# Moving the skip term into the lag-0 tap, generating masters in blocks of 3 and 5 chunks, and splitting the table sums: a kernel of gated attention and state-space convolution

## The chip, the cores and the metric

The kernel runs on one core of one Trainium2 chip. The metric is the device time of one execution in microseconds (us). A kernel was run several times in each round, and the medians below are over its runs, all of one state (no run stood out as slow). A profile was taken of one execution of each kernel. In it PE is TensorE (PEld its weight loads), DVE is VectorE, ACT is ScalarE, POOL is GpSimd, SP is SyncE, whose instruction stream issues most DMAs here. L977 is line 977 of that kernel's file, and so the same statement has other line numbers in another kernel.

## The reference, cut to what matters

```python
x = A_x                                        # 2048 tokens x 448
g = sigmoid((x * gate_w).sum(-1, keepdims=True))
# branch a: 16 query heads of 28, one key and one value head for all
q, k, v = x @ wq, x @ wk, x @ wv
a = softmax(q k^T / sqrt(28)) v @ wo
# branch b: a convolution along the tokens, one kernel K of length 2048 for each channel
dt = exp(log_dt); logdA = dt * (A_re + i A_im)             # 448 channels x 256 states
K[d, l] = Re( sum_n C[d,n] * exp(logdA[d,n] * l) * dt*B[d,n] )
y = causal_convolution(x, K)
b = y + x * Dskip                                          # the skip term
return g * a + (1 - g) * b
```

The skip term `x * Dskip` is a convolution with a kernel that is `Dskip` at lag 0 and zero elsewhere. So it may as well be added to `K[:, 0]`.

## The kernel before

Attention and convolution run side by side. The attention makes 410 batches of scores (two or three tiles of 128 keys x 512 queries). TensorE writes the scores to PSUM (the memory for its results), ScalarE takes the exponential, and TensorE multiplies with the values. The convolution works on 28 chunks of 16 channels. For each one, VectorE builds tables of powers, TensorE multiplies them to the kernel K ("kernel generation"), K goes to DRAM and comes back as a Toeplitz matrix `T`, and TensorE convolves. VectorE then multiplies by 1-g into `cst` (this I call the eviction). TensorE transposes that, and VectorE adds it to `O`, the output of all tokens in SBUF (the core's working memory).

**A list scheduler makes the order.** The program declares operations with an assumed duration and a priority. At build time a simulation picks, again and again, the operation that can start first, and in case of a tie the one of lower priority number. This fixes each engine's instruction order before the program runs; where an operation isn't ready in time, its engine waits:

```python
def el(n, rate=0.96, fix=69):          # assumed ns of a VectorE operation on n elements
    return fix + n / rate
class Prog:
    SEM_NS = 60                        # assumed ns for a semaphore to reach another engine
    SLACK = {"pe": 500.0, "dve": 300.0}
    SWITCH = 107.0                     # assumed ns when TensorE changes its tiling
    def schedule(self):
        ...
        while done < n:
            for e in ENG:
                for i in ready[e]:
                    r = max(rt[i], free[e])
                    ...
                    key = (r, o.pr, i)
                    if best is None or key < best[0]:
                        best = (key, e, i)
```

The code below is shortened: access patterns and bookkeeping are cut.

**Masters** are the powers exp(dt·A·2^k), k = 0 to 10, by repeated squaring in float32, for a block of four chunks at once. Each power is cast to bf16, and a negated copy of its imaginary part is written beside it:

```python
def masters(self, b):                       # sizes = [4] * 7
    for k in range(11):
        if k:
            tensor_tensor(msq, src_both(k-1), src_both(k-1), mult)          # 2*BW elements, BW = 128
            tensor_tensor(mst re, msq re, msq im, subtract)                 # BW
            scalar_tensor_tensor(mst im, src re, 2.0, src im, mult, mult)   # BW
        tensor_copy(mbf ..., src_both(k))                                   # 2*BW, float32 to bf16
        tensor_scalar(mbf ..., src im, -1.0, mult)                          # BW, the negated copy
```

**Tables** double five times for each chunk: two multiplies and one sum over n = 128, 256, 512, 1024 and 2048 elements.

```python
        tensor_tensor(d, a, mbf re, mult)        # n
        tensor_tensor(tmp, a, mbf im/-im, mult)  # n
        tensor_tensor(d, d, tmp, add)            # n: the negated copy makes one addition of both halves
```

**The skip term and the end of the program:**

```python
def skip(self):
    pg.dma(x and B_Dskip -> SBUF)                                      # 1.8 MB
    for i in range(16):                                                # 128 tokens each
        scalar_tensor_tensor(tv, tv, (1 - g), Dskip, mult, mult)       # 448 elements
        tensor_tensor(ov, ov, tv, add)                                 # O += ...
...
    self.skip()
    for tt in range(4): self.outp(3, tt, tt)      # the last output projection, O += g * (attention @ wo)
    for qc in range(4): self.store(qc)            # 512 tokens each
```

Each `store(qc)` writes 512 tokens of all 448 channels. It waits for everything that was added to these tokens: the projections of these tokens, the skip term, and the convolution of all 28 chunks, since a chunk adds 16 channels to all tokens. Two stores are issued by SP and two by ScalarE.

Of the kernel before, what the change touches and what calls it, by code (L numbers as in the profile page):

```python
# [11 lines left out]
P = 128  # L12

S = 2048
D = 448
# [280 lines left out]
class Kernel:  # L296
# [28 lines left out]
    def alloc(self):  # L325
# [32 lines left out]
        sizes = [4] * 7  # L358
# [3 lines left out]
        self.AO = [0, 4, 128, 132, 256, 384]  # L362
        self.BO = [448 + 128 * k for k in range(6)]
        self.MC = 448 + 5 * 128 + 64
# [11 lines left out]
        self.zero = sb("zero", 2, BF)  # L376
# [5 lines left out]
    def consts(self):  # L382
        pg = self.pg
        V = lambda b, off, n: b.v(0, P, off, [[1, n]])
        pg.op("pool", lambda e: e.memset(V(self.ident, 0, 136), 1.0), 200, wr=["id"])
        pg.op("pool", lambda e: e.affine_select(
            out=V(self.ident, 0, 136), in_=V(self.ident, 0, 136), compare_op=ALU.is_equal, fill=0.0,
            base=0, pattern=[[-1, 136]], channel_multiplier=1), 300, rd=["id"], wr=["id"])
        sm = self.small
        pg.op("dve", lambda e: e.tensor_reduce(V(sm, 0, 1), self.ident.v(0, P, 28, [[32, 4]]), AX.X, ALU.max),  # L390
              100, rd=["id"], wr=["s0"])
        pg.op("dve", lambda e: e.memset(V(sm, 3, 1), 0.5 * math.pi), 60, wr=["hpi"])
        ms = lambda buf, n, val, key, eng="dve": pg.op(eng, lambda e: e.memset(V(buf, 0, n), val), 60 + n / 3.8, wr=[key])
        pg.op("dve", lambda e: e.memset(V(self.kstg, 0, 256), 0.0), 100, wr=[("kst", 0)])
        ms(self.Wk, NT * P, 0.0, "Wk")
        ms(self.Wq, NT * 512, 0.0, "Wq")
        ms(self.Wb, P, 0.0, "Wb")
        for hb in range(4):
            pg.op("dve", lambda e, hb=hb: e.memset(self.Wb.v(32 * hb, 28, 32 * hb + 28, [[1, 1]]), -1.0), 60, wr=["Wb"])
        pg.op("dve", lambda e: e.memset(self.vaug.v(0, P, 28, [[32, 16]]), 1.0), 80, wr=["va"])  # L400
        pg.op("dve", lambda e: e.memset(self.vaug.v(0, P, 29, [[32, 16], [1, 3]]), 0.0), 80, wr=["va"])
        ms(self.Wo, NT * D, 0.0, "Wo", "pool")
        for zh in range(4):
            an = self.anti.v(0, 16, zh * P, [[32, 4], [1, 32]])
            pg.op("pool", lambda e, an=an: e.memset(an, 1.0), 100, wr=["anti"], pr=4)
            pg.op("pool", lambda e, an=an, zh=zh: e.affine_select(out=an, in_=an, compare_op=ALU.is_equal, fill=0.0,
                                                                  base=zh // 2 + zh % 2 - 32, pattern=[[0, 4], [1, 32]],
                                                                  channel_multiplier=2), 300,
                  rd=["anti"], wr=["anti"], pr=4)

    def loads(self):
# [32 lines left out]
        pg.op("dve", lambda e: e.tensor_copy(self.Wv.v(0, DT, 28, [[32, 4]]), self.smallb.v(0, DT, 0, [[1, 4]])), 80, rd=["smb"], wr=["Wv"])  # L444
        w = ins["A_wo"]
# [5 lines left out]

    def skip(self):
        pg, ins = self.pg, self.ins
        tab = self.xT
        keys = [("xT", hf, j) for hf in range(4) for j in range(2)]
        pg.dma([(tab.v(0, P, 0, [[D, 16], [1, D]]), dram(ins["A_x"], 0, [[D, P], [P * D, 16], [1, D]])),
                (tab.v(0, P, 16 * D, [[1, D]]), dram(ins["B_Dskip"], 0, [[0, P], [1, D]]))],
               (2176, 896), "xs", wr=["xs"] + keys, pr=4)
        for i in range(16):
            tv = tab.v(0, P, D * i, [[1, D]])  # L460
            ov = self.O.v(0, P, D * i, [[1, D]])
            pg.op("dve", lambda e, tv=tv, i=i: e.scalar_tensor_tensor(tv, tv, self.gtok.v(0, P, 16 + i, [[1, 1]]),
                                                                      tab.v(0, P, 16 * D, [[1, D]]), ALU.mult, ALU.mult),
                  el(D), rd=["gt", "xs"], wr=[("xg", i)], pr=90)
            pg.op("dve", lambda e, tv=tv, ov=ov: e.tensor_tensor(ov, ov, tv, ALU.add),
                  el(D, 1.92), rd=[("xg", i)], comm=[("O", i // 4)], pr=90)
# [221 lines left out]
    def masters(self, b):  # L688
# [5 lines left out]
        A0 = lambda lv: mo + (BC * (self.AO[lv] // 128 * 128) + self.AO[lv] % 128)  # L694
        pr = 51.5 + c0 if b else 1.4
# [12 lines left out]
        for k in range(11):  # L708
            ks = "sz" if k == 0 else ("ms", k % 2)
            lv, w8 = (k, 16) if k < 5 else (5, 8) if k == 5 else (k - 6, 16)  # L710
            ro, io = A0(lv), mo + BC * self.BO[lv]
            sp_, sn_ = io + 4, io
            if k > 5:
                ro, sp_, sn_ = ro + 8, io + 8, io + 12
            lk = ("mb", b % 2, k)
            if k:
# [10 lines left out]
            pg.op("dve", lambda e, k=k, ro=ro, sp_=sp_, w8=w8: e.tensor_copy(  # L727
                mbf.v(0, P, ro, [[sp_ - ro, 2], [w8, 8 * BC], [1, 4]]), src_both(k)),
                el(2 * BW, 1.92), rd=kk, wr=[lk], pr=pr)
            pg.op("dve", lambda e, k=k, sn_=sn_, w8=w8: e.tensor_scalar(  # L730
                mbf.v(0, P, sn_, [[w8, 8 * BC], [1, 4]]), src(k, 1), -1.0, None, ALU.mult),
                el(BW, 1.92), rd=kk, wr=[(lk, 1)], pr=pr)

    def tables(self, c):
# [14 lines left out]
        for lv in range(5):  # L749
            w = 1 << lv  # L750
            ra = mo + BC * (self.AO[lv] // 128 * 128) + self.AO[lv] % 128 + 128 * ci
            rb = mo + BC * self.BO[lv] + 128 * ci
            mk = [("mb", b % 2, lv), (("mb", b % 2, lv), 1), ("mb", b % 2, lv + 6), (("mb", b % 2, lv + 6), 1)]
            rk = [("tab", s, l) for l in range(lv + 1)]
# [6 lines left out]
                el(n, 1.92), rd=rk + mk, wr=[("tab", s, lv + 1)], pr=pr)  # L761
            pg.op("dve", lambda e, a=src, rb=rb, w=w: e.tensor_tensor(  # L762
                tmp.v(0, P, so, [[4 * w, 32], [1, 4 * w]]), a,
                mbf.v(0, P, rb, [[4, 32], [0, w], [1, 4]]), ALU.mult),
                el(n, 1.92), rd=rk + mk, wr=[("tmp", s)], pr=pr)
            t2 = tmp.v(0, P, so + 4 * w, [[8 * w, 16], [-4 * w, 2], [1, 4 * w]])
            pg.op("dve", lambda e, d=dst, t=t2: e.tensor_tensor(d, d, t, ALU.add), el(n, 1.92),  # L767
                  rd=[("tmp", s), ("tab", s, lv + 1)], wr=[("tab", s, lv + 1)], pr=pr)
        ra = mo + BC * self.AO[5] + 64 * ci
        rb = mo + BC * self.BO[5] + 64 * ci  # L770
        mk = [("mb", b % 2, 5), (("mb", b % 2, 5), 1)]
        rk = [("tab", s, l) for l in range(6)]
# [5 lines left out]
        pg.op("dve", lambda e: e.tensor_tensor(ub, src, mbf.v(0, P, rb, [[4, 16], [0, 32], [1, 4]]), ALU.mult),  # L778
              el(2048, 1.92), rd=rk + mk, wr=[("tab", s, 7)], pr=pr)

    def kgen(self, c):
# [5 lines left out]
        for jj, comp in ((jj, comp) for jj in range(4) for comp in range(2)):  # L787
            def mm(e, jj=jj, comp=comp):
                for half in range(2):
                    for g in range(4):  # L790
# [4 lines left out]
                            start=(comp == 0 and half == 0), stop=(comp == 1 and half == 1),  # L795
                            tile_position=(0, 32 * g), skip_group_check=True)
                return r
            pg.op("pe", mm, 165, rd=[("tab", s, l) for l in range(8)], wr=[X, ("kst", c % 2)], pr=1.9, mode="c32",
# [148 lines left out]
    def main(self):  # L947
# [92 lines left out]
        self.skip()  # L1040
# [52 lines left out]
```

## Time and profile before

| | before |
|---|---|
| median of the first 3 runs | 540.87 us (537.03 to 541.70) |
| span of the profiled execution | 537.2 us |
| busy PE / DVE / ACT | 90% / 90% / 91% |
| first exponential starts | 22.5 us |
| first start to end of the last exponential ("the stretch") | 497.0 us |
| end of the last exponential to the end of the span ("the tail") | 17.7 us |
| end of VectorE's last kernel-generation operation | 492.4 us |

The span falls into three pieces: before the first exponential, the stretch, the tail. A row of the timeline gives start in us, length, engine, line, operation, tile written and read, shapes, count. This is the timeline of the tail of before (start in us, length, engine, line, operation, tile written and read, shapes, count):

```profile
525.92 2.12 DVE L883 SCALAR_TENSOR_TENSOR O<-psS,gtok,O 128x448 bf16<-128x448 f32 x3
...
527.96 0.68 DVE L861 TENSOR_TENSOR cst<-psS,omq 128x512 bf16<-128x512 f32 x1
...
529.78 0.96 SPq L106 DMA_DIRECT2D out_dram<-O  x2
529.78 1.05 ACTq L106 DMA_DIRECT2D out_dram<-O  x2
```

The last projections are added (L883), then the last chunk is evicted (L861) and added, and only then, at 529.8 us, all four stores are issued at once. The span ends 7.4 us later.

These are three groups of VectorE in before (count, then busy us and mean ns of one), the operations that the change touches:

```profile
L767 DVE TENSOR_TENSOR tab<-tab,tmp 128x2048 bf16<-128x2048 bf16 x28 | 34.0, 1216 | 0.0
...
L727 DVE CAST mbf<-mst 128x256 bf16<-128x256 f32 x70 | 20.1, 288 | 0.1
...
L730 DVE TENSOR_SCALAR mbf<-mst 128x128 bf16<-128x128 f32 x70 | 15.3, 218 | 0.0
```

### The profile page before, as it was taken

How to read it: one execution, taken by the hardware profiler on the slowest of the kernel's cores; microseconds unless marked ns; L12 is line 12 of the kernel's file. 1: busy time of each engine (PE TensorE's matmuls, PEld its weight loads, DVE VectorE, ACT ScalarE, POOL GpSimd, SP SyncE). 2: the span in 40 equal slices, each digit the busy share in tenths (PEclk: the TensorE clock that was granted, in tenths of full speed). 3: DMA queues.
4: the chain of work that ended last, by engine and by line, in shares of the span. 5: the costliest groups of instructions: out<-in, count | busy, mean ns of one | idle time of the engine just before them, and what ended most of it. 6: DMA issues, size and time to landing. Idle time of an engine off the chain costs nothing.

```text
span 537.2 us, 18418 instructions
## 1 busy us (share of the span) xinstructions
PE 484.8 (90%) x8229; PEld 243.8 (45%) x8229; DVE 483.9 (90%) x1168; ACT 487.5 (91%) x428; POOL 4.9 (1%) x17
## 2 busy tenths in 40 slices
PE   6778888999999899999999999999999998998893
PEld 5411132553545444554545445554455543544452
DVE  4978899998999999999999999999999999999023
ACT  4599998998999999999999999999999999999960
POOL 3000000000000000000000000000000000000000
PEclk9855566997999999999999999999999999889997
DMA  8735445777798867779898896778877796697954
GB/s 232 145 79 137 138 139 207 245 285 299 249 327 297 303 230 237 253 265 345 304 337 320 262 332 238 242 260 319 309 296 267 285 393 220 176 388 254 350 188 137
DMA packets 42266, 138.16 MB, mean 257 GB/s; under 512 B 8168, under 2 KB 24476, under 8 KB 27852
## 3 DMA queue, kind: packets, MB, share of 16 engines
q1 hardware_dynamic: 40396, 135.71, 73.7%
q10 hardware_dynamic: 1792, 1.29, 0.8%
q8 instruction: 64, 1.05, 0.8%
q14 instruction: 14, 0.11, 0.1%
HBM read 133.01 MB, written 3.85 MB: 255 GB/s over the span
## 4 chain that ended last, share of the span: by engine, by line
PE 47%; ACT 36%; DVE 12%; DMA 2%; issue 1%; POOL 1%; DVEq 0%; POOLq 0%
ACT expT L977 35%; PE psS L967 13%; PE psS L853 12%; PE psB L985 8%; PE psX L792 6%; PE psX L676 2%; DMA T<-KP_scratch 2%; DVE tab L767 2%; DVE tmp L762 2%; DVE tab L759 2%; PE psS L504 1%; PE psX L877 1%; PE psX L831 1%; DVE O L883 1%; DVE tab L776 1%
## 5 line engine op out<-in xcount | busy, mean ns | idle before, releaser
L977 ACT ACTIVATE expT<-psS 128x1536 bf16<-128x1536 f32 (+1 forms) x410 | 470.8, 1254 | 19.0 <-PE psB L985 12.9
L967 PE MATMUL psS<-qT,kT 29*128 29x512 bf16 x1024 | 170.6, 412 | 29.6 <-ACT expT L977 27.2
L853 PE MATMUL psS<-T,U 128*26 128x128 bf16 (+7 forms) x3584 | 157.9, 303 | 0.6 <-DMA T<-KP_scratch 0.5
L853 PEld LDWEIGHTS psS<-T,U 128*26 128x26 bf16 (+7 forms) x3584 | 113.9, 152 | 35.3 <-issue 28.2
L985 PE MATMUL psB<-expT,vaug 128*32 128x512 bf16 x1024 | 108.8, 417 | 1.4 <-ACT gtok L643 1.3
L967 PEld LDWEIGHTS psS<-qT,kT 29*128 29x128 bf16 x1024 | 39.6, 92 | 124.4 <-ACT expT L977 92.8
L762 DVE TENSOR_TENSOR tmp<-tab,mbf 128x2048 bf16<-128x2048 bf16 (+4 forms) x140 | 78.0, 563 | 0.0
L759 DVE TENSOR_TENSOR tab<-tab,mbf 128x2048 bf16<-128x2048 bf16 (+4 forms) x140 | 77.9, 563 | 0.0
L767 DVE TENSOR_TENSOR tab<-tab,tmp 128x2048 bf16<-128x2048 bf16 (+4 forms) x140 | 77.8, 563 | 0.0
L792 PE MATMUL psX<-tab 128*32 128x96 bf16 x1792 | 54.8, 268 | 1.3 <-issue 1.2
L985 PEld LDWEIGHTS psB<-expT,vaug 128*32 128x32 bf16 x1024 | 26.6, 95 | 64.2 <-issue 60.8
L792 PEld LDWEIGHTS psX<-tab 128*32 128x32 bf16 x1792 | 41.2, 116 | 14.2 <-issue 9.0
L776 DVE TENSOR_TENSOR tab<-tab,mbf 128x2048 bf16<-128x2048 bf16 x28 | 34.0, 1216 | 0.0
L778 DVE TENSOR_TENSOR tab<-tab,mbf 128x2048 bf16<-128x2048 bf16 x28 | 34.0, 1213 | 0.0
L861 DVE TENSOR_TENSOR cst<-psS,omq 128x512 bf16<-128x512 f32 x28 | 19.0, 680 | 15.7 <-PE psS L853 15.5
L717 DVE TENSOR_TENSOR msq<-mst 128x256 f32<-128x256 f32 x63 | 26.2, 416 | 0.0
L676 PE MATMUL psX<-xT,Wq 112*128 112x512 bf16 x64 | 21.7, 436 | 0.4 <-DVE O L838 0.2
L727 DVE CAST mbf<-mst 128x256 bf16<-128x256 f32 x70 | 20.1, 288 | 0.1
L720 DVE TENSOR_TENSOR mst<-msq 128x128 f32<-128x128 f32 x70 | 19.7, 282 | 0.0
L723 DVE SCALAR_TENSOR_TENSOR mst<-mst 128x128 f32<-128x128 f32 x63 | 17.8, 283 | 0.0
L804 DVE TENSOR_REDUCE kstg<-psX 128x128 bf16<-128x256 f32 x28 | 11.7, 418 | 4.2 <-PE psX L792 4.1
L730 DVE TENSOR_SCALAR mbf<-mst 128x128 bf16<-128x128 f32 x70 | 15.3, 218 | 0.0
(112 smaller groups left out, 255.8 us busy)
## 6 DMA issues: line engine op xcount, KB each, us to landing
T<-KP_scratch SPq DMA_DIRECT2D x112, 1024.0 KB, 7.8
rdenB<-R_scratch SPq DMA_DIRECT2D x60, 64.0 KB, 3.8
U<-in_A_x_dram SPq DMA_DIRECT2D x3, 896.0 KB, 5.4
tab<-in_A_x_dram SPq DMA_DIRECT2D x4, 448.0 KB, 6.9
O<-Z_scratch SPq DMA_DIRECT2D x1, 1792.0 KB, 13.6
KP_scratch<-kstg SPq DMA_DIRECT2D x28, 64.0 KB
xT<-in_A_x_dram SPq DMA_DIRECT2D x1, 1792.0 KB, 9.2
U<-Z_scratch SPq DMA_DIRECT2D x1, 896.0 KB, 8.0
```

The source lines that it names most:

```text
L676: pg.op("pe", lambda e, T=T: e.matmul(px, self.Wq.v(0, DT, T * 512 + g * 128, [[1, 128]]), self.xT.v(0, DT, T * S + 512 * qc, [[1, 512]]), ...
L717: pg.op("dve", lambda e, k=k: e.tensor_tensor(msq.v(0, P, 0, [[1, 2 * BW]]) if k > 1 else msq.v(0, P, 0, [[BW, 2], [1, BW]]), src_both(k - ...
L759: pg.op("dve", lambda e, d=dst, a=src, ra=ra, w=w: e.tensor_tensor(d, a, mbf.v(0, P, ra, [[8, 16], [0, 2 * w], [1, 4]]), ALU.mult), el(n, ...
L762: pg.op("dve", lambda e, a=src, rb=rb, w=w: e.tensor_tensor(tmp.v(0, P, so, [[4 * w, 32], [1, 4 * w]]), a, mbf.v(0, P, rb, [[4, 32], [0, w ...
L767: pg.op("dve", lambda e, d=dst, t=t2: e.tensor_tensor(d, d, t, ALU.add), el(n, 1.92), rd=[("tmp", s), ("tab", s, lv + 1)], wr=[("tab", s, ...
L776: pg.op("dve", lambda e: e.tensor_tensor(ua, src, mbf.v(0, P, ra, [[8, 8], [0, 64], [1, 4]]), ALU.mult), el(2048, 1.92), rd=rk + mk, wr=[( ...
L778: pg.op("dve", lambda e: e.tensor_tensor(ub, src, mbf.v(0, P, rb, [[4, 16], [0, 32], [1, 4]]), ALU.mult), el(2048, 1.92), rd=rk + mk, wr=[ ...
L792: r = e.matmul(self.psX.v(32 * g, 32, 96 * jj, [[1, 96]]), tab.v(0, P, o + 768, [[4, 32]]), tab.v(0, P, o, [[256, 3], [4, 32]]), start=(co ...
L853: r = e.matmul(ps.v(32 * j, 33 - m, po + 128 * k, [[1, 128]]), self.U.v(0, P, (m - 1) * D + 4 * gi + j, [[D, 33 - m]]), self.T.v(0, P, s * ...
L967: r = e.matmul(self.psS.v(0, P, 1536 * s + 512 * k, [[1, 512]]), kT.v(32 * h, DH + 1, 128 * kt, [[1, 128]]), qT.v(32 * h, DH + 1, 512 * qs ...
L977: pg.op("act", lambda e: e.activation(expT.v(0, P, 512 * (i0 % 10), [[1, n]]), self.psS.v(0, P, 1536 * s, [[1, n]]), AF.Exp, scale=SQ), 75 ...
L985: r = e.matmul(self.psB.v(32 * h, 32, 0, [[1, 512]]), vaug.v(0, P, 32 * kt, [[1, 32]]), expT.v(0, P, 512 * ((4 * st + h) % 10), [[1, 512]] ...
```

## The change

The intent is to take work off VectorE. The skip term goes away as VectorE work: `Dskip` is held in one row of a zeroed tile, and four tiny matmuls for each chunk add it to the lag-0 column of K while K still lies in PSUM. So that they can add, the accumulation group covers the whole bank. Only the first matmul carries the start flag. The masters work on five chunks at a time (and three in the first block) and write real and imaginary parts interleaved, without the negated copy. The table sum then has to add in one half and subtract in the other: two instructions of n/2 in place of one of n. The masters of the next block are also spread over the present block's chunks by a new priority.

```diff
-        sizes = [4] * 7
+        sizes = [3, 5, 5, 5, 5, 5]
...
-    def skip(self):                      # with its load and its 32 operations
...
-        pr = 51.5 + c0 if b else 1.4
+            pr = 52.5 + self.blocks[b - 1][0] + (self.blocks[b - 1][1] - 1) * (k + 1) / 11.0 if b else 1.4
...
-                mbf.v(0, P, ro, [[sp_ - ro, 2], [w8, 8 * BC], [1, 4]]), src_both(k)),
-                el(2 * BW, 1.92), rd=kk, wr=[lk], pr=pr)
-            pg.op("dve", lambda e, ...: e.tensor_scalar(... src(k, 1), -1.0, None, ALU.mult),
-                el(BW, 1.92), rd=kk, wr=[(lk, 1)], pr=pr)
+                mbf.v(0, P, ro, [[dc, 2], [st, 8 * BC], [1, 4]]), src_both(k)),
+                el(2 * BW, 1.17), rd=kk, wr=[lk], pr=pr)
+            if k == 5:                   # one negated copy is left, for the last level
...
-            pg.op("dve", ... tensor_tensor(d, d, t, ALU.add), el(n, 1.92), ...
+            for k, (o0, ds, t0, ts, op) in enumerate(((0, 384, 4 * w, 4 * w, ALU.add), (128, 128, 0, 12 * w, ALU.subtract))):
+                pg.op("dve", ... tensor_tensor(d, d, t, op), el(n // 2, 1.92), ...
...
-                            start=(comp == 0 and half == 0), stop=(comp == 1 and half == 1),
+                            start=(jj == 0 and comp == 0 and half == 0), stop=False,
+                if jj == 3 and comp == 1:
+                    for g in range(4):
+                        r = e.matmul(self.psX.v(32 * g, 32, 95, [[96, 4]]), self.ident.v(0, P, 0, [[1, 32]]),
+                                     self.dsk.v(0, P, 16 * c + 4 * g, [[1, 4]]), start=False, stop=True, ...)
...
-        self.skip()
```

## The prediction

> **What bounds the kernel now.** I read the page's busy lines first, then busy shares in 40 slices, then the chain, then the groups of VectorE by shape, then the stretches, and at the end the order of instructions around the end.
>
> ```profile
> PE 484.8 (90%) x8229; PEld 243.8 (45%) x8229; DVE 483.9 (90%) x1168; ACT 487.5 (91%) x428; POOL 4.9 (1%) x17
> ...
> DVE  4978899998999999999999999999999999999023
> ACT  4599998998999999999999999999999999999960
> PEclk9855566997999999999999999999999999889997
> ...
> PE 47%; ACT 36%; DVE 12%; DMA 2%; issue 1%; POOL 1%; DVEq 0%; POOLq 0%
> ...
> L977 ACT ACTIVATE expT<-psS 128x1536 bf16<-128x1536 f32 (+1 forms) x410 | 470.8, 1254 | 19.0 <-PE psB L985 12.9
> ```
>
> Three engines stand at 90%, so the shares alone decide nothing. The end does: VectorE (third and fourth row) falls to 0 to 3 tenths in the last slices while ScalarE is still at 9. So VectorE is done early, and the 410 exponentials of the attention go on to 519.5 us. Where nothing disturbs them they follow each other at 1.12 us on the mean (26 of them take 29.12 us in the chain from 490.41), though the row says 1254 ns, because neighbours overlap. 410 x 1.12 = 459 us. The first starts at 22.5 us and the last ends at 519.5: 497 us. The 38 us of difference are some 8 us of other activations and table loads before 33.8 us, and about 30 us of gaps. Only those 30 us, the 22.5 us before and the 17.7 us after are to be had.
>
> What makes the gaps? The row above says that most of the visible ones end with a TensorE matmul. I compared every exponential's start to the next one's with 1331 ns (1536 columns) and 901 ns (1024), and looked at what TensorE did in between. The large excesses stand where much convolution or kernel-generation work was placed between two batches of scores: 40 matmuls and 1.5 us at 128 us (the granted clock was half there), 35 and 0.8 us at 177 us, 32 and 0.9 us at 460 us. So TensorE's fixed order, with clumps in it, costs the time; VectorE's part is small. Waits of TensorE for VectorE after 100 us add up to some 8 us, most under 0.5 us each, and few reach ScalarE: 20 kernel-generation matmuls with 0.8 us at 207 us, 26 with 0.9 us at 297 us. I put them at 3 us together.
>
> ```profile
> L462 DVE SCALAR_TENSOR_TENSOR xT<-xT,gtok 128x448 bf16<-128x448 bf16 x16 | 10.7, 674 | 0.0
> L465 DVE TENSOR_TENSOR O<-O,xT 128x448 bf16<-128x448 bf16 x16 | 6.1, 381 | 0.0
> ...
> 489.36 0.67 DVE L462 SCALAR_TENSOR_TENSOR xT<-xT,gtok 128x448 bf16<-128x448 bf16 x1
> 489.96 0.37 DVE L465 TENSOR_TENSOR O<-O,xT 128x448 bf16<-128x448 bf16 x1
> 490.26 0.67 DVE L462 SCALAR_TENSOR_TENSOR xT<-xT,gtok 128x448 bf16<-128x448 bf16 x1
> ...
> 500.00:520.00 20.00, 17.52 (x299) 8.90 (x298) 2.13 (x4) 19.53 (x18) 0.00 (x0) 1.00 0.90 306
> ```
>
> The first two rows are the skip term (16 + 16 operations). The next three, from the timeline, show that an operation costs its distance to the next one, 0.60 and 0.30 us, not its duration of 0.67 and 0.37. The skip runs from 445.0 to 495.1 us, in gaps of the table work. The last line (stretch, then busy PE, PEld, DVE, ACT, POOL) says that from 500 to 520 us VectorE works 2.1 of 20 us. A saving of VectorE work there buys nothing.
>
> **What the Trainium skill says.** "VectorE: DVE Perf Modes", section on the TRN2 errata, gives 58 cycles plus elements over the mode's factor, at 0.96 GHz, so about 60 ns fixed. Agrees: the bf16 table multiplies of 2048, 1024, 512, 256 and 128 elements start 1135, 602, 335, 202 and 135 ns apart here, which is 68 ns + n/1.92. Float32 squarings of 256 are 335 ns, 68 + n/0.96. Same page, "Mode 2×_2P": a one-source operation runs at two elements a cycle by giving each half of the outermost dimension its own port. The 256-element cast of the masters is 202 ns here, which agrees. "SBUF — State Buffer", section on the DMA port swizzle, says that SBUF is accessed in 16-byte cachelines and crossing to a new one pays; no row of before shows a price. The new cast puts real and imaginary parts, one port each by the rule above, in the same 16 bytes, so it may collide. "TensorE: Matmul & The Clock Gate", "Wait — 56ns, not 53.3ns?", says starts never come closer than about 25 ns however small the matmul. The 64-column transposes here load 16 weights in 0.33 us, 21 ns each, slightly below.
>
> **The change part by part.** VectorE distances, us:
> - Skip removed: 16 x (0.596 + 0.303) = 14.4 saved. Also a 1.8 MB load that starts at 429.5 us and lands 9.8 us later, beside loads of T. One zeroing of 448 elements at the start is added (0.2).
> - Masters now: one block is 10 x (335 + 202 + 202) + 11 x (202 + 136) = 11.1 us, seven blocks 77.8. After: five chunks give 160 columns for 128. Squaring 401, subtraction and product 235 each, cast 235, one negated copy 151: 10 x 871 + 11 x 235 + 151 = 11.4. Three chunks (96 columns): 268, 168, 168, 168, 118, so 8.0. Sum 5 x 11.4 + 8.0 = 65.2: 12.5 saved. If the cast collides and falls to about 1.2 elements per ns (my guess, also the rate the changed scheduler plans with), it is 340 in place of 235 and 55 x 0.105 + 0.7 = 6.5 of it are lost again.
> - Table sums split: the elements stay, 5 x 28 = 140 instructions more at 68 ns: 9.5 added.
> - The multiplies read another layout with the same counts; the first multiply already reads that pattern at full rate. 0.
> - Net: -14.4 - 12.5 + 9.5 = -17.4 of 484, or -11 with the collision.
>
> TensorE: 4 tiny matmuls for each of 28 chunks. 112 x 21 to 25 ns = 2.4 to 2.8 added, spread, about 0.1 each time. The accumulation flags cost nothing.
>
> On the path: the 17 us lie on an engine that ends 20 us early, so they don't come off the end. What can: part of the 3 us of stalls at kernel generation (masters are spread over the previous block's chunks, so tables come evenly: in the built order the chunks' kernels end every 30 to 35 score matmuls, where before they come in runs of 20 to 30 and then a pause of 50), say -2; the removed load near 430 to 440 us, where DMA is at 9 tenths, -1; a denser order of TensorE by the tiny matmuls, +1. The built order has as many overfull stretches as before: 35 gaps between batches hold 28 or more convolution matmuls (36 before), 25 hold 32 or more for kernel generation (26). So I leave the rest of the 30 us as it is.
>
> The tail: before, 16 groups of four convolution matmuls stand after the last attention product, after the change 24, 14 of them behind the last output projection (7 before). Groups go at 28 matmuls in 1.08 us, so 7 more are +1.1 behind it; one VectorE operation less stands between, -0.3. Tail +0.8. In return 8 groups less (1.2 us of TensorE) stand beside the exponentials: -0.7.
>
> Sum: -2 - 1 + 1 + 0.8 - 0.7 = -1.9. I add -2 as my choice, since the change was presumably kept for a reason and VectorE was wholly full from 240 to 440 us. 540.87 - 3.9 = 537.
>
> **The rivals.**
> - VectorE is the true bound between 160 and 490 us (40.0 of 40 us busy from 240 to 280; the chain goes through it from 399 to 453 us). Then most of the 17 us come off: about 524. Against it: ScalarE is busy 39.6 in that same stretch, so it has no 17 us to give.
> - Nothing moves, because TensorE's order and ScalarE fix the span: 539 to 541. For it: the equal counts of clumps.
> - The collision of the cast is worse than planned, the plan's TensorE order waits for tables that come late, and kernels slip: 543 to 548. For it: the order is fixed when built, and a late table stops TensorE and so the scores. Against: the plan has the slow rate in it.
>
> **Range and chances.** The three runs before span 537.0 to 541.7; a rebuilt order moves clumps by luck, about 4 us either way on 30 us of gaps. So 530 to 543, and 2% (below 530.1) only if the first rival holds at least in part: 0.11. Slower than 551.7 needs the last rival and more: 0.02.
>
> **What would show it.** Right: VectorE's busy time near 466 to 473 us; no skip rows; masters' cast at 235 or 340 ns; split sums at half the elements plus 68 ns; the tail from the last exponential to the end about 18.5 us; exponentials still filling 22 to 519 us less 1 to 4. Wrong: exponential gaps falling from 30 to 20 us or less (then VectorE, or its unevenness, was the cause), or TensorE waiting for tables by 5 us or more.

## The result, and the profile after

The median after is 533.46 us (533.11 to 534.47, four runs). The median before, with one more run of it, is 539.84 us. A ratio here is the mean time of one kernel's fast runs over that of the other's of the same rounds, and so it is not quite the ratio of the medians: 0.9889, with a 95% interval of 0.984 to 0.9939. (The record of this result has no line on correctness; experiments 8, 9 and 12, which do the same work, are recorded as correct.) The kernel is about 1.1% faster, inside 2%, and the time lies in the predicted range of 530 to 543, but below the predicted 537.

These are the page's lines of after that answer to those of before in the prediction (busy time; busy tenths in 40 slices; the chain by engine; the exponentials' group):

```profile
PE 475.1 (89%) x8326; PEld 245.4 (46%) x8341; DVE 469.9 (88%) x1165; ACT 486.4 (91%) x428; POOL 5.5 (1%) x17
...
DVE  3978899899999999999999999999999999993023
ACT  4598999999999999999999999999999999999960
...
PEclk9765566899999999999999999999999999999997
...
PE 41%; ACT 34%; DVE 21%; issue 1%; POOL 1%; POOLq 0%
...
L966 ACT ACTIVATE expT<-psS 128x1536 bf16<-128x1536 f32 (+1 forms) x410 | 469.7, 1260 | 14.2 <-PE psB L974 9.6
```

VectorE's busy time falls from 483.9 to 469.9 us, and it is done one slice earlier, as its row shows. The exponentials cost the same as before (469.7 us for 410), but the idle time before them falls from 19.0 to 14.2 us. VectorE's share of the chain rose from 12 to 21%, which one doesn't expect of an engine that was relieved. In the clock row before has a 7 in the slice from 121 us and two 8s from 457 to 483 us. After has nothing but 9 from 107 us to the last slice.

The groups of VectorE and TensorE in after that answer to those of before:

```profile
L751 DVE TENSOR_TENSOR tab<-tab,tmp 128x1024 bf16<-128x1024 bf16 x56 | 36.2, 687 | 0.0
...
L709 DVE CAST mbf<-mst 128x320 bf16<-128x320 f32 x50 | 16.3, 325 | 0.0
...
L783 PE MATMUL psX<-dsk,ident 128*32 128x4 bf16 x112 | 5.8, 188 | 0.0
```

Splitting the largest sum turns 28 instructions with 34.0 us into 56 with 36.2. The cast of 320 elements takes 325 ns where that of 256 took 288, and the negated copies are gone except one in eleven. The tiny matmuls are there, 112 of them. Their mean of 188 ns is a latency, and they overlap: four of them take 0.20 us from the first start to the last end. In 26 of the 28 chunks all four start within 6 to 31 ns (within 52 and 72 ns in the other two).

The tail of after, in the timeline:

```profile
521.63 1.93 PE L842 MATMUL psS<-T,U 128*28 128x128 bf16 x56
523.62 0.69 DVE L850 TENSOR_TENSOR cst<-psS,omq 128x512 bf16<-128x512 f32 x1
...
524.86 0.42 DVE L827 TENSOR_TENSOR O<-O,psX 128x256 bf16<-128x256 bf16 x1 [0.55 <-PE psX L820]
525.31 0.96 SPq L106 DMA_DIRECT2D out_dram<-O  x2
525.31 1.05 ACTq L106 DMA_DIRECT2D out_dram<-O  x2
```

56 convolution matmuls stand alone behind the last projection. Then come eviction, transposes and addition, and then all stores at once, 7.4 us before the end. So the tail has the same form as before.

The split of the two spans:

| us | before | after | difference |
|---|---|---|---|
| to the first exponential | 22.5 | 23.7 | +1.1 |
| the stretch | 497.0 | 490.7 | -6.3 |
| the tail | 17.7 | 18.5 | +0.8 |
| span | 537.2 | 532.7 | -4.5 |

Whether the change has a part in the later start isn't shown. The granted clock first fell to half at 22.6 us in before and at 21.0 us in after. But it did so at 19.8 us in experiment 4 below, which has the instruction order of before and starts at 23.1 us, and experiment 12, which has the whole change, starts at 22.5 us. The whole gain lies in the stretch. So the question is why the stretch got 6.3 us shorter when only 1 to 4 were expected, and what of it the removed work has brought.

Two stretches of equal length (start:end, length, then busy us and count of PE, PEld, DVE, ACT and POOL, then the granted clock, the DMA share and GB/s), first of before, then of after:

```profile
120.00:160.00 40.00, 38.09 (x697) 19.21 (x696) 38.30 (x82) 37.47 (x33) 0.00 (x0) 0.91 0.83 297
440.00:480.00 40.00, 36.81 (x673) 18.69 (x671) 38.54 (x77) 37.26 (x33) 0.00 (x0) 0.91 0.74 262
```

```profile
120.00:160.00 40.00, 36.63 (x705) 19.65 (x697) 39.72 (x99) 38.86 (x36) 0.00 (x0) 1.00 0.77 271
440.00:480.00 40.00, 38.39 (x749) 20.89 (x749) 38.94 (x86) 38.37 (x34) 0.00 (x0) 1.00 0.87 295
```

ScalarE gets 33 instructions done in 40 us of before, and 36 and 34 in after, and in both stretches of before the mean granted clock was 0.91. Read more finely, the clock of before was halved for 6.8 us from 125 us, and for 3.4 us each from 456 and 470 us. In after it was never halved between 100 us and the last exponential. "TensorE: Matmul & The Clock Gate", section "What's actually happening", says that the clock has just two states and that a free-running window of about 3.4 us decides. The lengths here, 3.4 and 6.8 us, agree with that. The windows before and in the first halving of before:

```profile
121.60:125.00 3.40, 2.29 (x18) 0.75 (x19) 3.40 (x5) 3.40 (x4) 0.00 (x0) 0.99 1.03 417
125.00:128.40 3.40, 3.40 (x36) 1.16 (x38) 2.78 (x4) 3.08 (x4) 0.00 (x0) 0.50 0.73 308
128.40:131.80 3.40, 3.40 (x50) 1.35 (x46) 2.48 (x9) 1.97 (x2) 0.00 (x0) 0.50 0.54 154
```

For 3.4 us TensorE is busy only 2.29 us, because ScalarE (3.40 of 3.40) is behind and TensorE waits for it. In the next 6.8 us the clock is half, the work that TensorE then has takes longer, and now ScalarE waits: 3.08 and 1.97 of 3.40. The two other halvings of before follow windows with 2.4 and 2.5 us of TensorE as well; there TensorE waits not for ScalarE alone but also 0.47 us for VectorE's eviction and 0.49 us for a transfer of `T`. But this doesn't happen each time: I laid windows of 3.41 us in that phase over the whole trace, and of the six of before with less than 2.5 us of TensorE three were followed by half a clock and three weren't, and after has three such windows with none. What decides it isn't shown. (In the kernel of experiment 2 one halving followed 2.8 us of TensorE.) ScalarE's longest idle times in or just behind these halvings of before are 1.4 us (to 130.7 us), 0.8 us (to 461.5) and 1.0 us (to 471.7): together 3.2 us, half of the 6.3. That is at most the part of the clock, for before also has an idle time of 1.0 us (to 313.6 us) at the full clock.

The waits themselves say more than the clock. From 100 to 512 us ScalarE waits for TensorE 11.9 us in before and 6.5 us in after; the 5.4 us between them are most of the 6.3. The larger group of these waits (engine, tile and line, what it waited for, us in total, times, longest), first of before, then of after:

```profile
ACT expT L977 <- PE psB L985: 9.5, 21, 1.4
```

```profile
ACT expT L966 <- PE psB L974: 6.0, 17, 0.9
```

In all fourteen profiles, those of the experiments below too, the stretch less the waits of ScalarE for TensorE is 483.5 to 486.8 us, while the stretches run from 490.6 to 500.6. The time at half clock doesn't follow the stretch so closely: between 100 us and the last exponential experiment 8 has 10.2 us of it, with waits of 6.6 us and a stretch of 491.1, and experiment 6 has none, with 11.4 and 495.3. A single profile's stretch is no better than some 2 us: experiments 1 and 6 have the same work in the same order up to the stores, and their stretches are 493.1 and 495.3 us.

### The profile page after: what moved, and what is told of

It is laid out like the page before. It is cut to its first block, busy times and chain, and to the rows that moved or that the text cites. A ratio compares the mean times of both kernels' runs of the same rounds, so it can differ in the third digit from the quotient of the medians.

```text
span 532.7 us, 18623 instructions
## 1 busy us (share of the span) xinstructions
PE 475.1 (89%) x8326; PEld 245.4 (46%) x8341; DVE 469.9 (88%) x1165; ACT 486.4 (91%) x428; POOL 5.5 (1%) x17
## 4 chain that ended last, share of the span: by engine, by line
PE 41%; ACT 34%; DVE 21%; issue 1%; POOL 1%; POOLq 0%
ACT expT L966 33%; PE psS L956 11%; PE psS L842 10%; PE psB L974 7%; PE psX L776 5%; DVE tab L751 4%; DVE tab L741 3%; DVE tmp L744 3%; PE psX L660 3%; DVE tab L759 2%; DVE tab L761 1%; PE psX L866 1%; PE psS L488 1%; DVE cst L850 1%; PE psX L820 1%
## 5 line engine op out<-in xcount | busy, mean ns | idle before, releaser
L966 ACT ACTIVATE expT<-psS 128x1536 bf16<-128x1536 f32 (+1 forms) x410 | 469.7, 1260 | 14.2 <-PE psB L974 9.6
L842 PE MATMUL psS<-T,U 128*32 128x128 bf16 (+7 forms) x3584 | 158.7, 302 | 2.3 <-issue 1.5
L842 PEld LDWEIGHTS psS<-T,U 128*32 128x32 bf16 (+7 forms) x3584 | 114.0, 152 | 31.8 <-issue 25.4
L751 DVE TENSOR_TENSOR tab<-tab,tmp 128x256 bf16<-128x256 bf16 (+3 forms) x280 | 90.0, 362 | 0.5
L741 DVE TENSOR_TENSOR tab<-tab,mbf 128x128 bf16<-128x128 bf16 (+4 forms) x140 | 79.8, 570 | 0.6
L744 DVE TENSOR_TENSOR tmp<-tab,mbf 128x128 bf16<-128x128 bf16 (+4 forms) x140 | 79.1, 566 | 0.0
L850 DVE TENSOR_TENSOR cst<-psS,omq 128x512 bf16<-128x512 f32 x28 | 19.2, 687 | 19.0 <-PE psS L842 18.7
L699 DVE TENSOR_TENSOR msq<-mst 128x320 f32<-128x320 f32 (+1 forms) x54 | 25.1, 465 | 0.0
L709 DVE CAST mbf<-mst 128x320 bf16<-128x320 f32 (+1 forms) x60 | 18.8, 314 | 0.0
L702 DVE TENSOR_TENSOR mst<-msq 128x160 f32<-128x160 f32 (+1 forms) x60 | 18.6, 310 | 0.0
L705 DVE SCALAR_TENSOR_TENSOR mst<-mst 128x160 f32<-128x160 f32 (+1 forms) x54 | 16.7, 309 | 0.0
L820 PE MATMUL psX<-ident,cst 128*64 128x64 bf16 x448 | 12.7, 198 | 4.5 <-DVE cst L850 3.0
```

Source lines behind the costliest of these rows:

```text
L699: pg.op("dve", lambda e, k=k: e.tensor_tensor(msq.v(0, P, 0, [[1, 2 * BW]]) if k > 1 else msq.v(0, P, 0, [[BW, 2], [1, BW]]), src_both(k - ...
L741: pg.op("dve", lambda e, d=dst, a=src, ra=ra, w=w: e.tensor_tensor(d, a, mbf.v(0, P, ra, [[8, 16], [0, 2 * w], [1, 4]]), ALU.mult), el(n, ...
L744: pg.op("dve", lambda e, a=src, ra=ra, w=w: e.tensor_tensor(tmp.v(0, P, so, [[4 * w, 32], [1, 4 * w]]), a, mbf.v(0, P, ra + 4, [[8, 16], [ ...
L751: pg.op("dve", lambda e, d=d, t=t2, op=op: e.tensor_tensor(d, d, t, op), el(n // 2, 1.92), rd=[("tmp", s), ("tab", s, lv + 1)], wr=[("ts", ...
L842: r = e.matmul(ps.v(32 * j, 33 - m, po + 128 * k, [[1, 128]]), self.U.v(0, P, (m - 1) * D + 4 * gi + j, [[D, 33 - m]]), self.T.v(0, P, s * ...
L966: pg.op("act", lambda e: e.activation(expT.v(0, P, 512 * (i0 % 10), [[1, n]]), self.psS.v(0, P, 1536 * s, [[1, n]]), AF.Exp, scale=SQ), 75 ...
```

## The experiments

My theory after reading the traces was: the stretch is shorter because of another built order (its clumps, its pauses and the halvings of the clock), and hardly because VectorE has less to do. Clumps are places where much convolution or kernel generation stands between two batches of scores in TensorE's order. Rival 1: VectorE's load is what counts, a little with each us removed. Rival 2: the gain comes from a single part of the change. Rival 3: the spreading of the masters removed the clumps. Twelve kernels tell these apart. Each group of four ran on one chip beside before, six runs for each kernel and eleven of before. Medians and ratios below are against the runs of before in the same rounds (539.12 us for the first four, 539.15 for the next, 539.51 for the last).

An earlier build of the skip-only kernel didn't fit in SBUF, so the row of `Dskip` lies in a buffer that is free after the seeds. A ballast that repeated the casts was a race, and one that repeats the squarings into unread space took its place.

### 1. The skip term alone

```diff
 # before.py
-    def skip(self): ...
+        # zeroed row tile, B_Dskip loaded into partition 31 of it
-                            start=(comp == 0 and half == 0), stop=(comp == 1 and half == 1),
+                            start=(jj == 0 and comp == 0 and half == 0), stop=False,
+                # and the four tiny matmuls of each chunk, as in after
-        self.skip()
```

> The kernel before with only the skip moved into the lag-0 tap (masters and sums as before; the skip row reuses a free buffer, as memory is short). VectorE distance sum falls by 14.4 us, TensorE gains 112 tiny matmuls. Theory V (the time follows VectorE's load): nearly all of the gain, 534 to 536. Theory E (the even spread of the masters' work lets TensorE be fed evenly, and that is the gain): 538 to 540, as the bunches stay. Theory O (a rebuilt order changes the time by luck): anything from 534 to 543, with no relation to VectorE's busy time.

Measured: 531.30 us (529.47 to 534.52), ratio 0.9859 [0.9826, 0.9893]. One part of the change alone is faster than before, and by its ratio not behind the whole change (0.9889; the intervals overlap). The split says why: stretch 493.1 us (4 less than before), tail 12.2 us (5.5 less). This is its tail:

```profile
515.24 0.69 DVE L856 TENSOR_TENSOR cst<-psS,omq 128x512 bf16<-128x512 f32 x1 [4.93 <-PE psS L848]
...
517.23 0.41 DVE L833 TENSOR_TENSOR O<-O,psX 128x256 bf16<-128x256 bf16 x1
...
517.67 0.95 SPq L106 DMA_DIRECT2D out_dram<-O  x2
517.67 7.19 ACTq L106 DMA_DIRECT2D out_dram<-O  x2
...
521.60 2.84 DVE L878 SCALAR_TENSOR_TENSOR O<-psS,gtok,O 128x448 bf16<-128x448 f32 x4
```

In this built order the last chunk is evicted (L856) at 515.2 us, before the last projections are added (L878, from 521.6 us). So three of the four stores can go at 517.7 us, beside the rest of the attention, and just the last one (the second of the ScalarE queue) waits, until 524.5 us. In before and after all four wait for the last chunk. The prediction doesn't have this term at all.

### 2. Masters and table sums alone

```diff
 # after.py
+    def skip(self): ...          # as before, and called as before
-                            start=(jj == 0 and comp == 0 and half == 0), stop=False,   # and no tiny matmuls
+                            start=(comp == 0 and half == 0), stop=(comp == 1 and half == 1),
```

> The changed kernel with the old skip at the end put back (no tiny matmuls). VectorE's sum is 3 us below before and 14.4 above the changed kernel. Theory V: 538 to 540. Theory E: 533 to 536. Theory O: anything from 534 to 543; here the built order leaves 37 groups of convolution matmuls (148) behind the last score matmul where the changed kernel has 24, so a tail longer by about 0.5 to 1.5 us under every theory.

Measured: 537.76 us (537.35 to 540.81), ratio 0.9992 [0.9961, 1.0023]: nothing. Its stretch is 492.0 us, 5 less than before, but its tail is 19.7 and its start 23.5 us. Single-profile splits and medians don't match to the microsecond, and the medians decide: this part alone brings nothing that these six runs can see.

### 3. After, with ballast on VectorE in the same order

```diff
 # after.py
-        self.msq = sb("msq", 2 * BW, F32)
+        self.msq = sb("msq", 4 * BW, F32)
-     tensor_tensor(msq.v(..., [[1, 2 * BW]]),                src_both(k - 1),        src_both(k - 1), mult)
+     tensor_tensor(msq.v(..., [[2 * BW, 2], [1, 2 * BW]]),   twice(src_both(k - 1)), twice(src_both(k - 1)), mult)
+     # the second copy is never read; the assumed duration stays, so all engines keep their order
```

> The changed kernel with every squaring of the masters done twice, the second time into unread space, without telling the scheduler: the same order on every engine, VectorE about 50 x 0.333 + 10 x 0.2 = 18.7 us more work (slightly more than before had). Theory V: back to 539 to 545. Theories E and O: little, 533 to 536, as the order on TensorE is the same; more only where a table comes late.

Measured: 543.88 us (541.21 to 545.04), ratio 1.0083 [1.0053, 1.0113], where after stands at 0.9889. By the pitch (the distance of one operation's start to the next one's) the ballast is 50 x 0.333 us + 10 x 0.2 us = 18.7 us; the busy time rose by 16.7. The time rose by 10.4 us over after, across rounds. The stretch went from 490.7 to 500.6 us. First the busy lines and the chain of the ballast kernel, then two of its waits from 100 to 512 us (engine, line, what it waited for, us in total, times, longest), then the same two waits of after:

```profile
PE 479.4 (88%) x8326; PEld 246.0 (45%) x8341; DVE 486.6 (90%) x1165; ACT 488.8 (90%) x428; POOL 5.5 (1%) x17
...
DVE 59%; PE 20%; ACT 18%; DMA 1%; issue 0%
```

```profile
PEld psX L825 <- DVE cst L855: 9.3, 13, 1.4
...
PEld psX L781 <- DVE tab L766: 3.5, 6, 0.8
```

```profile
PEld psX L820 <- DVE cst L850: 5.4, 11, 1.1
...
PEld psX L776 <- DVE tab L761: 1.3, 3, 0.8
```

With the ballast the chain runs through VectorE for 59% of the span. TensorE's weight loads wait for it 28.8 us in all from 100 to 512 us, where they wait 16.7 in after, and ScalarE waits for TensorE 13.7 us where it waits 6.5. So in the order of after, VectorE has at most some 8 us to spare (18.7 less 10.4, my subtraction). Work added to VectorE costs time; it isn't a free engine. By itself this would speak for rival 1.

### 4. Before, with the skip's operations emptied in the same order

```diff
 # before.py
-            tv = tab.v(0, P, D * i, [[1, D]])
-            ov = self.O.v(0, P, D * i, [[1, D]])
+            tv = tab.v(0, P, D * i, [[1, 4]])
+            ov = self.O.v(0, P, D * i, [[1, 4]])
```

> The kernel before with the same order on every engine, but the 32 skip operations cut to 4 columns each (wrong result on purpose). VectorE has 12 us less work, all of it between 445 and 495 us. If the skip work delayed anything (theory V): 536 to 538. My prediction's reading (a filler that delays nothing, and its load still runs here): within 1 us of before, 539 to 541.

Measured: 538.31 us (535.93 to 538.96), ratio 0.9978 [0.995, 1.0006]; stretch 494.5 us. The output is wrong, as intended. Taking the skip's elements out of the same order gains 0.2%, not told apart from zero; the median lies between the two ranges that were expected. By the pitch this is 11 us of VectorE: the two operations start 134 and 77 ns apart where they had 596 and 303. So VectorE's load in this order doesn't explain experiment 1's 1.4%.

### 5. After, built with the true rate of the cast

```diff
 # after.py: assumed durations only
-                el(2 * BW, 1.17), rd=kk, wr=[lk], pr=pr)
+                el(2 * BW, 1.92), rd=kk, wr=[lk], pr=pr)
-                    el(BW, 0.87), rd=kk, wr=[(lk, 1)], pr=pr)
+                    el(BW, 1.92), rd=kk, wr=[(lk, 1)], pr=pr)
```

> The changed kernel, only the scheduler's planned rate of the masters' cast and negated copy set to what the trace measured (1.92 elements per ns, 236 ns for 320; it had planned 1.17). No work changes, only orders. The built order now ends the last chunk's kernel after 943 score matmuls (960 before) and leaves 11 groups of convolution behind the last score, not 24, all ahead of the last output projection. Theory T (the end decides: a convolution that is done before the last projection lets three of the four stores go early, worth some 5 us, as the skip-only run showed): tail from the last exponential about 13 us in place of 18.4, whole time 526 to 530. Theory V (only VectorE's load counts): 533 to 535, as the load is the same. Theory O (luck): 530 to 538.

Measured: 537.05 us (533.24 to 538.43), ratio 0.9948 [0.9916, 0.9981]. The instructions are those of after, the assumed times are nearer to the measured ones (the cast's pitch is 236 ns, which is 68 + 320/1.92), and yet the kernel is 3.6 us slower than after by the medians (the two intervals overlap a little). The stretch is 497.5 us, the same as before's. The waits of ScalarE in this kernel between 100 and 512 us are back:

```profile
ACT expT L966 <- PE psB L974: 9.9, 21, 2.5
```

After has 6.0 us in 17 such waits, with 0.9 as the longest. The longest here, 2.5 us (365.6 to 368.0), isn't a clump: TensorE itself stood still for 1.34 us, to 366.1. The profile names no releaser; a transfer of `T` landed at 365.8 us, so it was probably that. Then the clock was halved for 3.4 us. The tail that the expectation's theory T forecast, about 13 us, came out as 16.6: the last chunk is evicted only at 526.6 us and the stores start at 529.3. A better plan by its own numbers gave a worse kernel, with the same work.

### 6. Skip alone, but with stores that wait for everything, in the same order

```diff
 # experiment 1's kernel
-                    (512, 896), f"out{qc}", rd=[("O", qc)], ...
+                    (512, 896), f"out{qc}", rd=[("O", k) for k in range(4)], ...
```

> The skip-only kernel with the same order on every engine, but each of the four stores waits until all of the output is complete, as they had to in before and after because the last convolution came last. Theory T: the tail grows from 12.2 to about 17 us, and the time from 531.3 to 535.5 or 536.5; that would be most of what that run gained. Theory V: 531 to 532, no change beyond 1 us.

Measured: 536.28 us (535.44 to 540.87), ratio 0.9960 [0.9928, 0.9991]; experiment 1 has 0.9859. The tail is 16.4 us in place of 12.2, and the stores are issued from 527.5 us. The ratio moves by 1.0%, 5 us; 4.2 of them are seen in the tail. So the early stores are worth most of what experiment 1 had over before. Without them the skip term alone stands at 0.9960, and the masters and sums alone (experiment 2) at 0.9992. So neither part alone is seen to bring the 1.1% (the intervals of this run and of the whole change just overlap), and nothing here speaks for rival 2.

### 7. Before, lightened by some 17 us in the same order

```diff
 # before.py, for blocks b >= 2 only
-    tensor_tensor(msq 2*BW, ...)      tensor_scalar(mbf BW, src im, -1.0)
+    tensor_tensor(msq 4, ...)         tensor_scalar(mbf 4, src im[0:4], -1.0)
```

> The kernel before in its own order on TensorE, ScalarE and the queues, but in blocks 2 to 6 the masters' squarings and negated copies are cut to 4 columns (wrong result on purpose): about 5 x (10 x 0.263 + 11 x 0.066) = 16.8 us less VectorE work, from some 130 us on. Theory V in its linear form (the ballast gave +10.4 us for +18.7 us): 9 us less, 530 to 531. My prediction's reading (VectorE's load is off the path, the order sets the gaps): 538 to 540. In between (the load counts only above a point where tables come late): 534 to 537.

Measured: 537.97 us (535.67 to 539.56), ratio 0.9976 [0.995, 1.0001]. Its output is wrong, which doesn't matter for the time. The busy line:

```profile
PE 485.7 (90%) x8229; PEld 243.8 (45%) x8229; DVE 470.4 (87%) x1168; ACT 487.5 (91%) x428; POOL 4.9 (1%) x17
```

VectorE's busy time is 470.4 us, the same as after's 469.9 (and by the pitch 50 x 0.262 + 55 x 0.065 = 16.7 us are gone), but the stretch is 497.7 us, as in before. This speaks against rival 1: a saving as large as after's, put into before's order, is worth 1.2 us by the medians, and its interval includes zero and ends at 0.5%.

### 8. After with the masters bunched again

```diff
 # after.py
-            pr = 52.5 + self.blocks[b - 1][0] + (self.blocks[b - 1][1] - 1) * (k + 1) / 11.0 if b else 1.4
+            pr = 51.5 + c0 if b else 1.4
```

> The changed kernel with the old priority of the masters, so that each block's masters run in a bunch again. Same work everywhere. Theory E (the even spread is a part of the gain): 536 to 540. Theory V: 533 to 535. Theory T: its built order leaves 84 convolution matmuls (21 groups) behind the last score, nearly the 24 of after, so the same tail and 533 to 535.

Measured: 534.32 us (533.11 to 537.31), ratio 0.9913 [0.9886, 0.9941]; stretch 491.1 us. The kernel is within 1 us of after. So the gain is there without the spreading of the masters, and rival 3 isn't needed. (It is also one more order of after's work, and orders alone move the time by some us, so a small part for the spreading isn't excluded.)

### 9. After, with the last chunk's convolution early

```diff
 # after.py: priority and slack of the convolution matmuls of the last chunk
-    pr=2.5,                              slack=(2500 if gi else 9000) if m == 1 else 0
+    pr=2.5 if c < NCH - 1 else 1.95,     slack=(9000 if gi == 0 else 2500 if c < NCH - 1 else 0) if m == 1 else 0
```

> The changed kernel with the last chunk's convolution put ahead of the waiting output projections; the order on TensorE is the same up to the last score matmul, only the tail is changed. Theory T (the tail is set by when the last convolution lets the stores go): the first three stores go some 2 to 3 us earlier against the last exponential, tail 15 to 16.5 us for 18.4, time 530 to 531.5. If the tail is set by the normalisation and the last projection alone: no change, 533 to 534.

Measured: 531.36 us (529.70 to 532.72), ratio 0.9859 [0.9824, 0.9894], after 0.9889. Stretch 490.6 us, as after; tail 16.1 in place of 18.5 us. Its tail:

```profile
520.67 0.68 DVE L850 TENSOR_TENSOR cst<-psS,omq 128x512 bf16<-128x512 f32 x1
...
523.15 0.96 SPq L106 DMA_DIRECT2D out_dram<-O  x2
523.15 1.84 ACTq L106 DMA_DIRECT2D out_dram<-O  x2
523.16 1.41 DVE L872 SCALAR_TENSOR_TENSOR O<-psS,gtok,O 128x448 bf16<-128x448 f32 x2
```

The eviction comes 3 us earlier than in after, and the last store alone waits for the last addition (until 524.6 us). The medians differ by 2.1 us and the tails by 2.4, so the size fits, though the two ratios' intervals overlap. It is the fastest version that has the whole change. It is level with experiment 1 (531.30). Both beat before; against after their lead of 2 us is within the overlap of the intervals.

### 10 to 12. The same work in other built orders

A constant of the scheduler's model was moved by a few nanoseconds, which changes no instruction, only the order in which they stand.

```diff
 # 10: before.py
-    SEM_NS = 60
+    SEM_NS = 64
```

```diff
 # 11: before.py, and 12: after.py
-    SWITCH = 107.0
+    SWITCH = 112.0
```

> The kernel before with the same work; only the scheduler's assumed semaphore delay is 64 ns for 60, so the order is rebuilt. Theory O (the order that before happens to have is a poor one, and a rebuilt one changes the exponentials' stretch by some us by luck): off 539 by 2 us or more, most likely faster, 533 to 537. Theory V or E: 538 to 540.5.

> As the run before it, by another constant: the assumed price of a switch of TensorE's tiling is 112 ns for 107. Theory O: a third value, 532 to 541, not the same as the one of the other order by 2 us or more. Theory V or E: 538 to 540.5, like before.

> The changed kernel with the same work, rebuilt with the switch priced at 112 ns. Its built order has 100 convolution matmuls behind the last score, 96 after the change. Theory O: 530 to 538, off 533.5 by up to 4 us. If the change itself, not its order, brings the gain: 532.5 to 535.

| kernel | median us (range) | ratio to before [95%] | stretch | tail |
|---|---|---|---|---|
| 10: before's work, order b | 535.14 (533.05 to 535.95) | 0.9923 [0.9888, 0.9958] | 490.9 | 18.3 |
| 11: before's work, order c | 537.04 (535.54 to 537.77) | 0.9961 [0.9927, 0.9994] | 493.3 | 18.2 |
| 12: after's work, order c | 538.02 (536.44 to 538.38) | 0.9973 [0.9937, 1.0010] | 495.6 | 18.6 |

Four nanoseconds in a constant make before's own work 4.4 us faster by the medians, with a stretch of 490.9 us, as after. Five nanoseconds in another make after's work as slow as before within the interval. So the order alone can move the time by about as much as the whole change did (4.4 and 6.4 us by the medians, with overlapping intervals). Experiment 12 lies at the very edge of the 530 to 538 that the theory of the order allowed, and 11 is 1.9 us from 10 where 2 or more were expected.

All orders of the same work together, leaving out those whose tail I altered on purpose: before's work has 539.5, 537.0 and 535.1 us (mean 537.2), after's 538.0, 537.1, 534.3 and 533.5 (mean 535.7). The means are 1.5 us apart, and each set is scattered over 4.4 or 4.6 us. So by these seven kernels the change apart from its order is worth some 1.5 us, which such a scatter can't tell from zero.

## Why the prediction was right or wrong

**The bound.** The prediction said that VectorE's saving lies on an engine that isn't the bound, and that the exponentials with the gaps that TensorE's fixed order makes are. Right, as experiments 4 and 7 show in the order of before: 11 and 17 us of VectorE less gave 0.2% each, not told apart from zero. The rival "VectorE is the true bound", with 524 us, is out. But the picture was one-sided. Experiment 3 shows that the spare room in the order of after is some 8 us at most: 18.7 us added there cost 10.4. The prediction's sentence that VectorE's part in the gaps is small holds for taking work away in before's order, not for adding work in after's.

**VectorE's sums.** Predicted net -17.4 us by the pitch and a busy time of 466 to 473 us; measured 469.9, 14.0 less than before. The split sums start 602, 335, 202, 136 and 102 ns apart for 1024, 512, 256, 128 and 64 elements. That is the predicted 68 ns + n/1.92. The squarings take 401, subtraction and product 235, the negated copy about 151 ns, as predicted. The cast with real and imaginary parts in the same 16 bytes is at 236 ns for 320 elements. The collision that I thought possible (340 ns), and that the changed scheduler plans with, doesn't happen. Right.

**The tiny matmuls.** Predicted 2.4 to 2.8 us spread, no visible cost. Four take 0.20 us with their latency. The estimate of 21 to 25 ns each was too dear, for the four start within 6 to 31 ns in nearly all chunks. It took the 0.33 us of the 16 weight loads of a transpose as 16 distances, but that time runs to the last one's end; in before the last 16 start within 0.22 us, in pairs 1 to 4 ns apart. VectorE's read of K now waits for the tiny matmuls, 4.4 us in all 28 chunks, where it waited 4.1 us for the last large ones. So no visible cost was right as far as this goes; they were not removed alone.

**The stalls at kernel generation, -2 us.** Wrong. They didn't shrink: from 100 to 512 us the matmuls and weight loads of kernel generation wait for VectorE 1.9 us in before and 2.9 in after. All matmuls wait for VectorE 1.6 us and all weight loads 13.2 us in before (the prediction read some 8 us in all), 4.1 and 16.7 in after. What shrank are the waits of ScalarE for TensorE, from 11.9 to 6.5 us.

**The removed load, -1 us, and the denser order, +1 us.** Open. No run takes the load away alone; experiment 4, which keeps it, and experiment 1, which doesn't, differ in their orders as well.

**The tail, +0.8 us.** Measured +0.8 (17.7 to 18.5 us), in the way that was worked out: more convolution groups behind the last projection. Right for this order. But the prediction took the tail as a length of TensorE work only. It missed that the four stores, 7.4 us of it, hang on the last chunk. Experiments 1, 6 and 9 show this term: 2 us (9 against after) to 5 us (6 against 1).

**The stretch.** Here the sum was mis-sized. The prediction counted overfull stretches of TensorE's order, found as many as before, and so left "the rest of the 30 us as it is", 1 to 4 us less. Measured 6.3 less. The step that failed is the one from equal counts of clumps to equal gaps, and in its place ScalarE's waits for TensorE fell by 5.4 us. Why the counts didn't tell is only argued: they don't say how a clump falls against the scores that ScalarE still has, nor that a pause of TensorE can be followed by half a clock. In before this happened three times, next to idle times of ScalarE of 1.4, 0.8 and 1.0 us; in after never. The prediction had the mechanism ("a rebuilt order moves clumps by luck, about 4 us either way") in the range and not in the centre. That is why the range held: 533.46 is 3.5 us below 537.0. (Some 1 us of this is the start of the sum: with the fourth run before's median is 539.84, not 540.87.) The four orders of after's work run from 533.5 to 538.0 us, with a mean of 535.7, and 537 would have been a fair guess for an unknown one of them.

**The -2 us "as my choice"**, because a kept change is presumably better than its sum, went in the right direction. By experiments 10 to 12 it can be read like this: whoever keeps the change that measured best keeps its lucky order with it. This is argued, not shown.

**What stays open.** How much of the 6.4 us is the work and how much the order. Three orders of one and four of the other give 1.5 us for the work, with a scatter three times that. More orders would narrow it. Also open is why a pause of TensorE is followed by half a clock in one case and not in another. One profile for each kernel doesn't tell whether the same pauses have it in each execution.

## What to carry to other kernels

When a scheduler fixes the order at build time, build both versions in several orders (a few nanoseconds in a constant of its model are enough) before you credit a change with a per cent: here before's own work ran in 535 to 539.5 us. Test an engine's load in the same order, by emptying or doubling its operations, in both directions: 17 us less in before's order bought 1 us, not told apart from zero, and 19 us more in after's cost 10. And ask of the end which transfers hang on the last piece of which work: letting the last chunk come a little earlier, or having it early by luck, was worth 2 to 5 us, more than the 1 to 1.5 us seen for the VectorE work that the change was about.

## What the Trainium skill lacked or had wrong

- "TensorE: Matmul & The Clock Gate", section "What's actually happening", ties the half clock to an idle window of about 3.4 us. Here it fell to half in the middle of the kernel after windows in which TensorE was busy 2.3 to 2.5 of 3.4 us, for 3.4 or 6.8 us (in experiment 2 also after 2.8 us of TensorE), and other windows with the same share were followed by the full clock. The page gives no busy share from which such a window keeps the full clock.
- No page says what it costs when the two halves of a one-source VectorE operation are written into the same 16 bytes. The cast here does that with real and imaginary parts, four bf16 elements each, and pays nothing: 236 ns for 320 elements, 68 ns + 320/1.92.
- "VectorE: DVE Perf Modes", TRN2 errata, gives 58 cycles of fixed cost, 60 ns at 0.96 GHz. The pitches here fit 68 ns.
